# One transfer for the output projection's weights, and one loop of filler matmuls ahead of it, in a decode kernel

## The chip, the cores and the metric

The kernel runs on one core of a Trainium2 chip. The metric is the device time of one execution in microseconds (us), as the median of several runs. A core has five engines, each with its own instruction stream, and they meet only at semaphores: PE (matmuls), DVE and ACT (elementwise work and copies), POOL, and SP, which here issues transfers. Transfers run on 16 DMA rings (one per DMA engine), each of which works off its queue in order.

## The reference, cut to what matters

One token of width 512 goes through a layer norm. Two branches read the result, and everything is added up:

```python
def _A_ref(x, k_cache, v_cache, wq, wo):      # attention, 32 heads on 8 kv heads
    q = (x @ wq).reshape(B, Sq, Hq, Dh)
    k, v = last 4096 positions of the caches, each kv head for 4 heads
    p = softmax(q k * Dh ** -0.5)
    o = p v
    return o.reshape(B, Sq, Hq * Dh) @ wo     # wo: 4096 x 512

def _B_ref(x, w_r, w_gate, w_up, w_down):     # one gated MLP, F = 1792
    r = x @ w_r
    g = silu(x @ w_gate); u = x @ w_up
    y = (g * u) @ w_down                      # w_down: 1792 x 512
    return x + y * sigmoid(r)

xn = layernorm(x)
out = x + _A_ref(xn, ...) + _B_ref(xn, ...)
```

All inputs are bf16. The weights and the two cache windows make 30.67 MB, each byte of which is read once.

## The kernel before

Everything is loaded by transfers that SP issues in this order: wq in two halves, the keys in four pieces of 2 MB, the values in four of 2 MB, w_gate, w_up, then wo in two transfers of 2 MB, and w_down in four pieces of 896, 512, 256 and 128 KB. The place of wo and w_down (`k_sb`) is that of the keys, so SP waits at L407 for DVE to have copied most of them out before it issues these six (L408 to L413, through the helper `dma` at L200, which gives each transfer a semaphore of its own).

In wo, `"(p j) n -> p (j n)"` puts 32 rows of 1 KB, 32 KB in all, on each of 128 partitions. `wo_chunks` cuts these at row 16, so that each transfer has 128 pieces of 16 KB.

PE goes through the stages one after another. The query projection (L300) and the keys' stage (loop at L397, transposes at L380 and scores at L389) come first, then the softmax and the values' stage (loop at L484). Then PE does the gate and up products (L524) and one small matmul, L529, which brings the attention's result into `oT2`. The end of the program is what the change touches:

- `warm(n)` (L189) issues n matmuls of zeros, 128x128 by 128x512, into a PSUM bank that nobody reads; `fill(n)` (L193) is two of them n times. They are called fillers here. They wait for nothing but their turn on PE.
- After L529 come four fillers (`fill(F4)`), and PE waits for `oT2`.
- The loop at L555 goes over the two pieces of wo. For each, PE waits for the piece and issues 16 matmuls (`grouped`, L546). A matmul has one column of `oT2` as its weights and one row of wo, 512 wide, as its moving data; its place `c = j % 4` puts four of them side by side in the array. Between the two pieces a loop of 8 rounds issues 16 fillers.
- When the 32nd matmul is done, DVE adds the four partial sums' bank and the residual (`t_part`, L565). PE issues four more fillers meanwhile.
- The loop at L567 goes over the four pieces of w_down. For each piece PE waits for it and issues two matmuls per row (`by_halves`, L551, 256 wide each). Behind the first piece's 14 it waits for DVE's sum and adds it through the same accumulators with `sel4` as weights.
- DVE and ACT copy the two halves of the result out (L578, L579), and SP writes it.

The order on each engine is the order of the calls in the source.

Of the kernel before, what the change touches and what calls it, by code (L numbers as in the profile page):

```python
# [38 lines left out]
def kernel(  # L39
# [63 lines left out]
    def early(eng, name, out_, in_):  # L103
        s = nc.alloc_semaphore("d_" + name)
        ins = eng.dma_start(out=out_, in_=in_)
        ins.then_inc(s, 16)
        ahead[ins.ins.name] = ins.ins.engine
        return (s, 16)

    t_wq = [early(nc.sync, "wq0", wq_sb[:, 0:KH, :], wq_v[:, 0:KH, :])]  # L110
    t_x = early(nc.scalar, "x", xrow[:], A_x.rearrange("a b d -> (a b) d"))
    W3, F1, F2, F3, F4 = 2, 2, 1, 1, 2

    sb = lambda name, shape, dt: nc.alloc_sbuf_tensor(name, shape, dt)
    HP = HKV // 2
# [71 lines left out]
    te, ac, ve, gp, sy = nc.tensor, nc.scalar, nc.vector, nc.gpsimd, nc.sync  # L187

    def warm(n):  # L189
        for _ in range(n):  # L190
            te.matmul(ps[:, 7, :], lhsT=zst[:], rhs=zmov[:], start=True, stop=True)  # L191

    def fill(n):  # L193
        warm(2 * n)
# [5 lines left out]
    def dma(eng, name, out_, in_):  # L200
        s = S("d_" + name)
        ins = eng.dma_start(out=out_, in_=in_)  # L202
        ins.then_inc(s, 16)
        if name == "v0":
            ends(ins)
        return (s, 16)
# [199 lines left out]

    SP.need((s_c[1], 6))  # L407
    wo_v = A_wo.rearrange("(p j) n -> p (j n)", j=RJ)  # L408
    wo_chunks = [(0, 16), (16, 32)]
    t_wo = [dma(sy, f"wo{k}", wo_sb[:, j0 * D:j1 * D], wo_v[:, j0 * D:j1 * D]) for k, (j0, j1) in enumerate(wo_chunks)]  # L410
    wd_v = B_w_down.rearrange("(p j) n -> p (j n)", j=FB)
    wd_chunks = [(0, 7), (7, 11), (11, 13), (13, 14)]
# [125 lines left out]
                                           in1=ps[:, 3, 0:FC].rearrange("p (i b) -> p b i", b=FB), op0=ALU.mult, op1=ALU.mult))  # L538
    DVE.need(t_h)
    t_hT = DVE.mark(ve.transpose(out=hTr[:].rearrange("p b i -> p (b i)"), in_=h4[:].rearrange("p b i -> p (b i)")))  # L540
    fill(F4)
    PE.need(t_oT2)

    def grouped(j, lhsT, w):
        c = j % 4
        return te.matmul(a_ps[32 * c:32 * c + 1, :], lhsT=lhsT, rhs=w[:, j * D:(j + 1) * D], start=(j < 4), stop=False,  # L546
                         tile_position=(0, 32 * c), skip_group_check=True)
# [7 lines left out]
    for k, (j0, j1) in enumerate(wo_chunks):  # L555
        PE.need(t_wo[k])
        for j in range(j0, j1):
            ins = grouped(j, oT2[:, j:j + 1], wo_sb)
        if k == 0:
            with te.Fori(0, 8):  # L560
                fill(1)
    t_g4 = PE.mark(ins)
    DVE.need(t_g4, t_rf)
    fill(2)
    t_part = DVE.mark(ve.tensor_tensor(out=part, in0=a_ps, in1=rf, op=ALU.add))  # L565
    PE.need(t_hT)
    for k, (j0, j1) in enumerate(wd_chunks):  # L567
# [45 lines left out]
```

## Time and profile before

| what | us |
|---|---|
| median of 8 runs (lowest, highest) | 79.0 (78.72, 79.25) |
| the profiled execution, device time | 78.94 |
| its span, from the first instruction to the last | 77.4 |
| PE busy, of the span | 59.3 |
| DVE busy | 44.0 |
| ACT busy | 30.4 |
| POOL busy | 10.1 |
| data read by DMA | 30.67 MB, 396 GB/s over the span |

The span leaves out some 1.5 us at the two ends of the profiled execution. Busy times are sums over an engine's instructions, without overlap counted twice; matmuls are pipelined, so PE busy does not say how far PE is from its peak. An engine can be busy for much of the span and still set nothing: what counts is what the last instruction waited for. "Issue to landing" of a transfer contains the time it stands in its ring behind others: the four pieces of w_down are issued near 34 us and take some 40 us to land.

### The profile page before, as it was taken

What the parts mean: (1) busy time and instruction counts of PE and PEld (TensorE: products, weight loads), DVE (VectorE), ACT (ScalarE), POOL (GpSimd) and SP (SyncE); (2) the same over time, 40 slices, a digit from 0 to 9 for tenths busy, and PEclk for the clock granted to TensorE, in tenths of its full rate; (3) what the DMA queues carried; (4) which work ended last, traced back from release to release, by engine and by line L of the source; (5) the groups of instructions that cost most, each with busy time, mean ns of one, the idle gap of its engine ahead of it and who ended that gap; (6) DMA issues with size and microseconds to landing.
All of it is one profiled execution on the core that took longest, in us unless ns stands there. A gap on an engine that the chain in (4) does not pass through costs nothing.

```text
span 77.4 us, 1669 instructions
## 1 busy us (share of the span) xinstructions
PE 59.3 (77%) x652; PEld 29.9 (39%) x652; DVE 44.0 (57%) x96; ACT 30.4 (39%) x41; POOL 10.1 (13%) x22
## 2 busy tenths in 40 slices
PE   0015996798898997997995866788887795798891
PEld 0010411336675775685682225222222251343240
DVE  2764900119866957966963762988989248300302
ACT  2771001402895896896775043333343420000001
POOL 3950000000220210220217600000000000000000
PEclk9999999999999999999999999999999999999999
DMA  5999999999999999999999999999989999999910
GB/s 136 389 424 406 406 423 508 423 406 406 415 474 440 415 415 406 432 491 415 410 406 415 432 474 423 415 420 415 459 370 487 422 415 415 423 419 399 379 39 1
DMA packets 2601, 30.72 MB, mean 397 GB/s; under 512 B 291, under 2 KB 422, under 8 KB 806
## 3 DMA queue, kind: packets, MB, share of 16 engines
q1 hardware_dynamic: 2594, 30.67, 94.1%
q8 instruction: 2, 0.03, 0.2%
q14 instruction: 1, 0.01, 0.0%
q10 hardware_dynamic: 4, 0.00, 0.0%
HBM read 30.67 MB, written 0.00 MB: 396 GB/s over the span
## 4 chain that ended last, share of the span: by engine, by line
DMA 70%; PE 14%; ACT 6%; DVE 3%; issue 2%; SPq 1%
DMA k_sb<-in_B_w_down_dram 51%; DMA k_sb<-in_A_k_cache_dram 20%; PE ps L380 8%; ACT kT L352 6%; PE ps L551 3%; PE ps L389 3%; DVE kin L344 2%; SPq L202 1%; DVE kT L349 1%; DVE kT L578 1%; SPq L84 0%; SPq L101 0%
## 5 line engine op out<-in xcount | busy, mean ns | idle before, releaser
L352 ACT COPY kT<-ps 128x1024 bf16<-128x1024 bf16 x19 | 18.6, 1016 | 8.8 <-PE ps L380 8.6
L380 PE MATMUL ps<-perm_bf,kin 128*128 128x128 bf16 x256 | 17.1, 220 | 0.9 <-DVE kin L344 0.4
L380 PEld LDWEIGHTS ps<-perm_bf,kin 128*128 128x128 bf16 x256 | 14.3, 98 | 5.2 <-issue 4.4
L344 DVE COPY kin<-k_sb 128x2048 bf16<-128x2048 bf16 x16 | 11.0, 691 | 4.7 <-DMA k_sb<-in_A_k_cache_dram 4.1
L191 PE MATMUL ps<-zmov,zst 128*128 128x512 bf16 x45 | 11.9, 396 | 1.2 <-PEq L84 1.2
L349 DVE COPY kT<-ps 128x1024 bf16<-128x1024 bf16 x13 | 9.0, 691 | 2.7 <-PE ps L380 2.2
L475 ACT CAST pvS<-ps 128x512 bf16<-128x512 f32 x8 | 4.7, 585 | 10.0 <-PE ps L481 10.0
L389 PE MATMUL ps<-kT,qAB 128*32 128x512 bf16 x68 | 6.8, 389 | 1.9 <-ACT kT L352 1.9
L337 POOL COPY qAB<-qpad 128x64 bf16<-128x64 bf16 x8 | 3.6, 448 | 31.8 <-PE ps L389 31.8
L191 PEld LDWEIGHTS ps<-zmov,zst 128*128 128x128 bf16 x45 | 3.9, 99 | 6.2 <-issue 3.3
L455 DVE COPY vin<-v_sb 128x2048 bf16<-128x2048 bf16 x8 | 5.5, 685 | 1.1 <-PE ps L490 1.0
L461 DVE COPY vin<-v_sb 128x2048 bf16<-128x2048 bf16 x8 | 5.5, 683 | 0.0
L490 PE MATMUL ps<-vin,pTcur 128*32 128x512 bf16 x32 | 3.2, 386 | 2.6 <-ACT pvS L475 2.2
L579 ACT CAST kT<-ps 1x256 bf16<-1x256 f32 x1 | 0.4, 363 | 11.9 <-PE ps L551 11.9
L502 PE MATMUL ps<-zmov,zst 128*128 128x512 bf16 x16 | 4.7, 376 | 0.0
L254 PE MATMUL ps<-ident_bf,xn_row 1*128 1x1 bf16 x4 | 0.3, 165 | 5.2 <-DVE xn_row L249 5.2
L300 PE MATMUL ps<-wq_sb,xnT 128*1 128x512 bf16 x32 | 3.8, 621 | 0.6 <-DMA wq_sb<-in_A_wq_dram 0.6
L565 DVE TENSOR_TENSOR kT<-ps,kT 128x512 f32<-128x512 f32 x1 | 0.7, 692 | 5.6 <-PE ps L546 5.6
L306 ACT CAST q<-ps 128x512 bf16<-128x512 f32 x2 | 1.2, 585 | 5.9 <-PE ps L300 5.9
L496 PE MATMUL ps<-vin,pTcur 128*32 128x512 bf16 x32 | 3.2, 387 | 0.3 <-DVE vin L461 0.2
L490 PEld LDWEIGHTS ps<-vin,pTcur 128*32 128x32 bf16 x32 | 1.1, 92 | 6.0 <-DVE vin L455 5.5
L389 PEld LDWEIGHTS ps<-kT,qAB 128*32 128x32 bf16 x68 | 1.9, 92 | 3.9 <-issue 1.4
(92 smaller groups left out, 52.5 us busy)
## 6 DMA issues: line engine op xcount, KB each, us to landing
k_sb<-in_A_k_cache_dram SPq DMA_DIRECT2D x4, 2048.0 KB, 22.4
v_sb<-in_A_v_cache_dram SPq DMA_DIRECT2D x4, 2048.0 KB, 38.4
wq_sb<-in_A_wq_dram SPq DMA_DIRECT2D x2, 2048.0 KB, 9.1
k_sb<-in_A_wo_dram SPq DMA_DIRECT2D x2, 2048.0 KB, 35.2
wq_sb<-in_B_w_gate_dram SPq DMA_DIRECT2D x1, 1792.0 KB, 42.8
wq_sb<-in_B_w_up_dram SPq DMA_DIRECT2D x1, 1792.0 KB, 46.7
k_sb<-in_B_w_down_dram SPq DMA_DIRECT2D x1, 896.0 KB, 39.1
k_sb<-in_B_w_down_dram SPq DMA_DIRECT2D x1, 512.0 KB, 39.9
```

The costliest lines, as they stand in the source:

```text
L191: te.matmul(ps[:, 7, :], lhsT=zst[:], rhs=zmov[:], start=True, stop=True)
L300: ins = te.matmul(ps[32 * c:32 * c + 1, hf, :], lhsT=xnT[:, kt:kt + 1], rhs=wq_sb[:, kt, (4 * hf + c) * 512:(4 * hf + c + 1) * 512], start ...
L344: ve.tensor_copy(out=kin[:, 2 * h:2 * h + 2, :], in_=k_sb[:, g, 2 * h:2 * h + 2, :]).then_inc(s_c[h], 1)
L349: ve.tensor_copy(out=kT[:, b, :], in_=tp[:, b, :]).then_inc(s_ev[b], 1)
L352: ac.copy(out=kT[:, b, :], in_=tp[:, b, :]).then_inc(s_ev[b], 1)
L380: ins = te.transpose(tp[:, b, k * P:(k + 1) * P], kin[:, b, k * P:(k + 1) * P], perm_bf[:])
L389: ins = te.matmul(sc[32 * cq:32 * cq + 32, e, :], lhsT=qAB[:, e, :], rhs=kT[:, b, :].rearrange("d (k h q) -> d h k q", h=2, q=PH)[:, e], s ...
L455: ve.tensor_copy(out=vin[:, 0].rearrange("p (q k) d -> p q (k d)", q=4), in_=v_in[:, :, 0:4 * DH]).then_inc(s_va, 1)
L461: ve.tensor_copy(out=vin[:, 1].rearrange("p (q k) d -> p q (k d)", q=4), in_=v_in[:, :, 4 * DH:]).then_inc(s_vb, 1)
L475: ac.copy(out=pvS[:].rearrange("p t d -> p (t d)"), in_=pv_ps).then_inc(s_pvs, 1)
L490: ins = te.matmul(pv_ps[32 * tl:32 * tl + 32, :], lhsT=pTcur[:, tl].rearrange("p q e r -> p (q e r)"), rhs=vin[:, 0].rearrange("p (q t) d ...
L502: te.matmul(ps[:, 7, :], lhsT=zst[:], rhs=zmov[:], start=True, stop=True)
```

## The change

`wo_chunks` becomes one piece of 32 rows, so wo is one transfer of 4 MB in 128 pieces of 32 KB, with one semaphore. The loop at L555 then runs once: one wait, and 32 matmuls behind it. The three places with fillers (4, then 16 in a loop between the pieces of wo, then 4) become one loop of twelve rounds of two, 24 again, directly behind L529 and ahead of the wait for `oT2`.

```diff
-    W3, F1, F2, F3, F4 = 2, 2, 1, 1, 2
+    W3, F1, F2, F3 = 2, 2, 1, 1
...
-    wo_chunks = [(0, 16), (16, 32)]
+    wo_chunks = [(0, 32)]
...
-    fill(F4)
+    with te.Fori(0, 12):
+        fill(1)
     PE.need(t_oT2)
...
         PE.need(t_wo[k])
         for j in range(j0, j1):
             ins = grouped(j, oT2[:, j:j + 1], wo_sb)
-        if k == 0:
-            with te.Fori(0, 8):
-                fill(1)
     t_g4 = PE.mark(ins)
     DVE.need(t_g4, t_rf)
-    fill(2)
     t_part = DVE.mark(ve.tensor_tensor(out=part, in0=a_ps, in1=rf, op=ALU.add))
```

## The prediction, made before the changed kernel ran

> **What bounds the kernel now.** I read the page first, for the shares of the engines and of the DMA.
>
> ```profile
> span 77.4 us, 1669 instructions
> DMA  5999999999999999999999999999989999999910
> q1 hardware_dynamic: 2594, 30.67, 94.1%
> DMA 70%; PE 14%; ACT 6%; DVE 3%; issue 2%; SPq 1%
> ```
>
> The DMA row is at nine tenths or more from the second slice to the last but two, and one queue (SP's) carries it all. So the span is the time that 30.67 MB take, plus a short head and tail. The second view is the chain that ended last, in order of time (start, length, what):
>
> ```profile
> 34.09 39.14 DMA k_sb<-in_B_w_down_dram
> 73.23 0.14 issue
> 73.36 1.80 PE ps L551 x26
> 75.16 0.01 issue
> 75.17 0.61 PE ps L551 x6
> 75.78 0.02 issue
> 75.81 0.41 DVE kT L578
> ```
>
> The first piece of w_down, issued at 34.09 and queued behind everything else, lands at 73.23; then PE works the 32 matmuls of L551 off. The third view is the timeline from 64 us on (start, length, engine, line, idle time before it and what ended it):
>
> ```profile
> 64.02 1.02 PE L191 MATMUL ps<-zmov,zst 128*128 128x512 bf16 x4
> 66.28 1.03 PE L546 MATMUL ps<-k_sb,oT 128*1 128x512 bf16 x16 [1.24 <-DMA k_sb<-in_A_wo_dram]
> 67.25 3.63 PE L191 MATMUL ps<-zmov,zst 128*128 128x512 bf16 x16
> 71.08 1.03 PE L546 MATMUL ps<-k_sb,oT 128*1 128x512 bf16 x16 [0.21 <-DMA k_sb<-in_A_wo_dram]
> 72.05 1.04 PE L191 MATMUL ps<-zmov,zst 128*128 128x512 bf16 x4
> 72.17 0.69 DVE L565 TENSOR_TENSOR kT<-ps,kT 128x512 f32<-128x512 f32 x1 [5.56 <-PE ps L546]
> ...
> 74.12 0.60 PE L551 MATMUL ps<-kT,sel 128*1 128x256 f32 x4
> 74.52 0.35 PEld L551 LDWEIGHTS ps<-k_sb,hTr 128*1 128x1 bf16 x8 [0.30 <-DMA k_sb<-in_B_w_down_dram]
> ...
> 75.17 0.09 PEld L551 LDWEIGHTS ps<-k_sb,hTr 128*1 128x1 bf16 x4 [0.31 <-DMA k_sb<-in_B_w_down_dram]
> 75.49 0.08 PEld L551 LDWEIGHTS ps<-k_sb,hTr 128*1 128x1 bf16 x2 [0.23 <-DMA k_sb<-in_B_w_down_dram]
> ```
>
> Inside what the chain calls PE work, PE waits for DMA three more times (0.30, 0.31, 0.23 us): each last piece of w_down is late for it. **The end is set by the last landing**, not by PE. The trace's records of the increments with which the 16 DMA rings report their shares give the landings: gate and up at 56.95 and 61.24, wo at 66.14 and 71.04, w_down at 73.23, 74.47, 75.13 and 75.45. They also show that a landing is that of one late ring: 14 rings end the last piece by 74.15, one at 74.97 and one at 75.45. The latest lost 1.35 us at 23.78, where a 16 KB packet of the instruction queue ran on it (1021 ns, and 1114 ns for the data packet after it); the other 0.86 us after an 8 KB instruction packet at 37.86.
>
> **The change, part by part.** *Transfer.* Two wo transfers of 128 pieces of 16 KB become one of 128 pieces of 32 KB; each ring has 8 packets fewer, and one increment fewer (9 ns). What a packet costs beyond its bytes: packets of 16384, 14336, 7168 and 1024 B took 611, 539, 274 and 46 ns (medians). From 14336 to 7168 B that is 0.0370 ns a byte, which leaves 9 ns a packet; from 16384 to 1024 B 0.0368 and 8 ns; from 16384 to 14336 B alone 0.0352 and 35 ns. So 8 x 8 + 9 = 0.07 us to 8 x 35 + 9 = 0.29 us less on the path. No row has a packet of 32 KB. If the hardware cuts it into two of 16 KB, only the 9 ns go; a loss is bounded by a rate as low as the slowest undisturbed 2 MB step of the queue, 4.91 us against 4.90, two of them 0.02 us. I take 10 ns a packet, **-0.09 us**, because the two wide pairs of sizes agree; ends +0.02 and -0.29.
>
> [...]
>
> *SP's queue.* One issue fewer (0.33 and 0.43 us now) lets the four w_down issues go some 0.4 us earlier, near 33.7. What hides it: the ring is 28 us behind (up lands at 61.24), the last w_down issue stands blocked for 12.85 us, and SP then has nothing until the output at 76.2. Cost 0; if the ring were empty it would be a gain of 0.4.
>
> *The 16 matmuls that ran on the first half.* They now wait for the whole wo, 71.04 - 0.09 = 70.95, and queue behind that wait with the other 16 and all of L551. Four run at a time in the four column groups: 16 take 1.03, a single one 0.378, so a further group of four costs (1.03 - 0.378) / 3 = 0.217, and 32 take 0.378 + 7 x 0.217 = 1.90. They run 71.0 to 72.9. DVE's sum at L565 follows 0.06 later as now, 72.96 to 73.65; it ended at 72.86 before, so it is **0.79 us later**. Who waits for it is the matmul with sel4, fifteenth in PE's order; it began at 74.12, after the 14 of the first w_down piece. That piece lands at 73.14, its 14 matmuls issue until about 73.9, after the sum is ready. So the 0.79 lies in a cover of 74.0 - 72.86 = 1.1 us, and behind it stand the 0.84 us of waits. Cost 0; past the cover each 0.1 us late would first eat those waits.
>
> *The fillers.* 4 + 16 + 4 become 24 in a loop, (16 in 3.63, so 0.217 each) 0.38 + 23 x 0.217 = 5.37 us, 64.02 to 69.4. They end 1.55 us before wo lands; they need not be waited for. The four behind wo, which ran until 73.09, held up nothing (w_down came at 73.23), and gone they give nothing. What they might have protected is the speed of PE. The clock row does not show it: the granted clock is 1.00 throughout, yet the same matmul shape takes 0.63 us early and 0.38 late:
>
> ```profile
> L300 PE MATMUL ps<-wq_sb,xnT x32: 585/631/634, 8.3 to 13.4; 128*1 128x512 bf16 x32
> L546 PE MATMUL ps<-k_sb,oT x32: 377/378/379, 66.3 to 71.7; 128*1 128x512 bf16 x32
> ```
>
> (L300 runs in two groups of 16, 1.88 us each.) After 15 us every matmul is fast, and the emptiest 3.4 us in that part are busy 60% (at 45.5) and 64% (from 63, with the gap of 1.24). After the change the emptiest are 69.4 to 72.8: 1.8 of 3.4 us, 53%. That is only a little outside what was endured; I price it at 0 and keep the slow clock as a rival.
>
> [...]
>
> **Sum.** -0.09 + 0 + 0 + 0. The profiled execution took 78.94 (span 77.4 and 1.5 around it) and would take 78.85; the runs shown have a median of 79.0, 0.06 above it, so **78.9**.
>
> **Rivals.** *First, slower: PE falls to its early speed in the gap before wo.* Place: 69.4 to 71.0. Price: at 1.88 for 16 and 0.63 for one, a group of four costs 0.42, and 32 take 0.63 + 7 x 0.42 = 3.6, so to 74.6; the sum of L565 ends at 75.35 and not 73.65. If PE recovers at once after, L551 has its sel4 (0.4) and 7 more pairs (0.11 each, from 14 in 0.93) left: 76.7 for 75.77, +1.0. If it stays slow, the 14 pairs at 0.21 and sel4 at 0.9 follow from 74.4: 78.3, +2.5. Time 80.0 to 81.5. It decides once L565 ends later than about 74.5 (73.9 plus the waits). For it: the emptiest stretch, and no full-array work after 69.4. Against: 1.24 us of gap and 64% left no mark. Chance 0.11.
>
> *Second, slower: an instruction packet falls on the late ring.* PE's program is 16 instructions shorter and the fetch seen at 74.28 (16 KB, 1264 ns, on a ring that was done) may come at another time. On the latest ring it would cost up to the 1.35 us of the fetch at 23.78, on the next 0.86 - 0.48. Time 79.3 to 80.2. Against: everything up to 64 us is the same code. Chance 0.08.
>
> *Third, faster: the latest ring is not delayed.* The end would be that of the next ring, 0.48 earlier, with the 0.09: 78.4. For it: the fetches hit rings by timing, and one run's trace cannot say how steady that is; against: the one at 23.78 lies long before the change. Chance 0.14.
>
> *Fourth: the change does not do what it says*, the pieces of 32 KB run as two of 16: 79.0. Chance 0.07.
>
> **How the numbers follow.** The forecast keeps 0.60, with its own range of 78.7 to 79.1 (-0.29 and +0.02, and 0.1 for the medians). A measurement of this kernel cannot tell less than about 0.3% (0.24 us) from no change. Of the 0.60, 0.10 lie below 78.76 by the 35 ns, 0.03 above 79.24. Faster: 0.10 + 0.14 = 0.24. Slower: 0.03 + 0.11 + 0.08 = 0.22. Same: 0.47 + 0.07 = 0.54. The range is 78.4 to 79.5: it leaves out the clock rival, half of the second and a little under 78.4, some 0.18.
>
> **What would show it.** Right: the one wo transfer lands near 70.9, 32 matmuls at 0.38 us begin there and end near 72.9, L565 ends near 73.65 and nobody waits for it, the three waits of L551 for w_down are still there, the last w_down piece lands near 75.35. Packets of 32 KB in the records at about 1215 ns confirm the saving; packets of 16 KB the fourth rival. Wrong: matmuls of 0.6 us after 71, a wait of L551 for L565 beyond 74.1, or a last ring that is late by something other than 1.3 us.

## The result, and the profile after

| | before | changed |
|---|---|---|
| median, us (lowest, highest) | 79.02 (78.72, 79.25), 52 runs | 78.78 (78.58, 79.07), 18 runs |
| ratio, 95% interval | | 0.9971 [0.9962, 0.9979] |
| profiled execution, us; its span | 78.94; 77.43 | 78.78; 77.36 |

The changed kernel is 0.24 us faster (0.17 to 0.30). Two more sittings on other occasions gave 0.9989 [0.9978, 1.0000] and 0.9975 [0.9961, 0.9989], so the gain is some 0.1 to 0.3%. The ratios leave out executions over 1.5% above the fastest of their kernel, and those among them in which the granted clock of PE fell (0.978 on average over the span) are counted by themselves below, because they are part of what the change touches.

The page of the changed kernel, the lines that answer to those of before:

```profile
span 77.4 us, 1676 instructions
DMA  5999999999999999999999999999999979799910
...
q1 hardware_dynamic: 2450, 30.67, 94.1%
DMA 71%; PE 14%; ACT 6%; DVE 3%; issue 2%; SPq 1%
```

SP's queue has 144 packets fewer: 128 of data and 16 increments. The DMA row is as full as before but for two sevens between 62 and 68 us, while wo runs, and the shares of the chain are the same to a per cent. The chain's end, in order of time (start, length, what):

```profile
33.66 39.51 DMA k_sb<-in_B_w_down_dram
73.17 0.14 issue
73.30 1.80 PE ps L552 x26
75.10 0.03 issue
75.13 0.59 PE ps L552 x6
75.73 0.02 issue
75.75 0.41 DVE kT L575
```

Each piece lies 0.06 us earlier than before (73.17 for 73.23, 75.75 for 75.81). The w_down issue stands at 33.66 for 34.09, as SP has one issue fewer, and nothing comes of that. The main lines of the changed kernel's timeline from 64 us on:

```profile
64.06 5.34 PE L191 MATMUL ps<-zmov,zst 128*128 128x512 bf16 x24
71.10 1.90 PE L547 MATMUL ps<-k_sb,oT 128*1 128x512 bf16 x32 [1.70 <-DMA k_sb<-in_A_wo_dram]
73.05 0.69 DVE L562 TENSOR_TENSOR kT<-ps,kT 128x512 f32<-128x512 f32 x1 [6.39 <-PE ps L547]
73.30 0.93 PE L552 MATMUL ps<-k_sb,hTr 128*1 128x256 bf16 x14 [0.30 <-DMA k_sb<-in_B_w_down_dram]
74.06 0.60 PE L552 MATMUL ps<-kT,sel 128*1 128x256 f32 x4
74.46 0.35 PEld L552 LDWEIGHTS ps<-k_sb,hTr 128*1 128x1 bf16 x8 [0.30 <-DMA k_sb<-in_B_w_down_dram]
...
75.13 0.09 PEld L552 LDWEIGHTS ps<-k_sb,hTr 128*1 128x1 bf16 x4 [0.33 <-DMA k_sb<-in_B_w_down_dram]
75.43 0.08 PEld L552 LDWEIGHTS ps<-k_sb,hTr 128*1 128x1 bf16 x2 [0.21 <-DMA k_sb<-in_B_w_down_dram]
```

The fillers end at 69.40, PE idles 1.70 us, the 32 matmuls take 1.90 us at full speed, and DVE's sum ends at 73.74, before sel4 wants it at 74.06. The three waits for w_down stand as before (0.30, 0.33, 0.21). So PE still waits for DMA to the end, and the gain in the span is that of the stream.

The stream, that is the work of SP's queue, is best read where only wo differs: from the landing of w_up to the landing of wo, by the increments of the slowest ring (differences taken before rounding). The table has the values of the kernels of the experiments below, too.

| kernel | wo transfers, piece | w_up to wo, us |
|---|---|---|
| before | 2, 16 KB | 61.24 to 71.04: 9.79 |
| e2, e11 (fillers alone) | 2, 16 KB | 9.79, 9.79 |
| e4, e10 | 1, 16 KB | 9.79, 9.79 |
| changed; e5, e9 | 1, 32 KB | 61.25 to 70.97: 9.71; 9.71, 9.72 |
| e1, e3, e8, e12 | 1, 32 KB | 9.71, 9.71, 9.71, 9.72 |
| e7 | 4, 8 KB | 9.93 |

The packets of 32 KB exist and took 1218 ns (median), against 2 x 611. So each of the eight on a ring saves 4 ns by the medians and some 9 ns by the table, and the whole saves 0.07 to 0.08 us. That is about a third of this sitting's gain, and more of the two smaller ones. The rest is what the experiments were for.

### The profile page after: what moved, and what is told of

Its sections match the earlier page's. It is cut to its first block, busy times and chain, and to the rows that moved or that the text cites. A ratio compares the mean times of both kernels' runs of the same rounds, so it can differ in the third digit from the quotient of the medians.

```text
span 77.4 us, 1676 instructions
## 1 busy us (share of the span) xinstructions
PE 58.1 (75%) x652; PEld 30.0 (39%) x652; DVE 43.9 (57%) x96; ACT 30.3 (39%) x41; POOL 10.5 (14%) x22
## 4 chain that ended last, share of the span: by engine, by line
DMA 71%; PE 14%; ACT 6%; DVE 3%; issue 2%; SPq 1%
DMA k_sb<-in_B_w_down_dram 51%; DMA k_sb<-in_A_k_cache_dram 20%; PE ps L380 8%; ACT kT L352 6%; PE ps L552 3%; PE ps L389 3%; DVE kin L344 2%; DVE kT L349 1%; SPq L202 1%; DVE kT L575 1%; SPq L84 0%; SPq L101 0%
## 5 line engine op out<-in xcount | busy, mean ns | idle before, releaser
L300 PE MATMUL ps<-wq_sb,xnT 128*1 128x512 bf16 x32 | 2.9, 500 | 0.7 <-DMA wq_sb<-in_A_wq_dram 0.7
L547 PE MATMUL ps<-k_sb,oT 128*1 128x512 bf16 x32 | 1.9, 378 | 1.7 <-DMA k_sb<-in_A_wo_dram 1.7
```

## Experiments

Unless said otherwise the diffs are against the changed kernel.

**e1: the transfer alone, four fillers left behind wo.**

```diff
-    with te.Fori(0, 12):
+    with te.Fori(0, 10):
         fill(1)
...
     DVE.need(t_g4, t_rf)
+    fill(2)
```

> One transfer of wo as in the changed kernel, but four of the 24 fillers stay behind wo as before, 20 stand ahead. The changed kernel measured -0.24 us (interval -0.17 to -0.30) while the two traces put only -0.07 us on the DMA stream. Packet theory (the gain is the wider pieces alone, and the rest of the -0.24 is how the timing of instruction fetches fell): -0.07 to -0.24, like the changed kernel. Filler theory (the four fillers behind wo cost the missing 0.17): -0.07, so slower than the changed kernel by 0.17. The sum of L565 follows the 32nd matmul by 0.06 either way, and the first w_down matmul starts when its piece lands, near 73.2, or when the four fillers are done, 0.87 after the 32nd matmul, near 73.9, whichever is later: if the second, up to 0.7 of the waits for w_down are eaten, and the end moves little.

Measured: 80.84 us, ratio 1.0234 [1.0212, 1.0256]; neither theory. The row of the granted clock on its page, which is all nines before:

```profile
PEclk9999999999999999999999999999999999995699
```

The stretches of its end (length, then busy time and count on PE, PEld, DVE, ACT, POOL, granted clock, DMA share, GB/s):

```profile
64.40:68.90 4.50, 4.50 (x25) 1.89 (x21) 2.34 (x4) 0.00 (x0) 0.00 (x0) 1.00 0.86 369
68.90:71.20 2.30, 0.03 (x5) 0.05 (x7) 0.00 (x0) 0.00 (x0) 0.00 (x0) 1.00 0.97 400
71.20:74.70 3.50, 3.50 (x33) 1.05 (x34) 0.00 (x0) 0.00 (x0) 0.00 (x0) 0.51 0.70 267
74.70:78.20 3.50, 3.04 (x36) 1.56 (x36) 1.11 (x2) 0.36 (x1) 0.00 (x0) 1.00 0.01 2
```

And of its timeline:

```profile
71.18 3.52 PE L547 MATMUL ps<-k_sb,oT 128*1 128x512 bf16 x32 [2.27 <-DMA k_sb<-in_A_wo_dram]
...
74.74 0.69 DVE L563 TENSOR_TENSOR kT<-ps,kT 128x512 f32<-128x512 f32 x1 [7.70 <-PE ps L547]
75.61 0.63 PEld L552 LDWEIGHTS ps<-k_sb,hTr 128*1 128x1 bf16 x14 [0.42 <-DVE kT L563]
```

This is the prediction's first rival, met by accident: with 20 fillers ahead the gap before wo is 2.26 us and not 1.70. The clock records of this trace put half clock from 71.30 to 74.71, exactly 3413 ns. In the 3413 ns before that PE was busy from 67.88 to 68.92 and from 71.18, 34% of the time. The 32 matmuls took 3.52 us (the rival's sum: 3.6), DVE's sum ended at 75.43 (the rival: 75.35), DMA waits vanish from L552, and the end lies at 78.2 for 76.2. All four executions have a granted clock of 0.978 or 0.979 on average, which is what one such stretch makes (half of 3.413 us is 0.0215 of the span of 79.4 us). The full clock came back after it, and the price was +1.9 us against before, four fillers behind wo included, between the rival's +1.0 and +2.5. As a test of the transfer by itself the run is lost.

**e2 and e11: the fillers alone.** Two transfers, all 24 fillers ahead.

```diff
-    wo_chunks = [(0, 32)]
+    wo_chunks = [(0, 16), (16, 32)]
```

> Two transfers of 16 KB pieces as before, all 24 fillers ahead of wo as in the changed kernel. Packet theory: 0.0 against before (78.97 to 79.07), as the stream is the same and PE waits for it. Filler theory: -0.17, most of the change's gain. Program-length theory (a PE program 15 instructions shorter moves instruction fetches): -0.17 too, to be told apart by the padded kernel.

> Two transfers of 16 KB pieces, all fillers ahead, none behind. Stream theory: as before, +0.0 (in the first six it was +0.1). Clock theory: in the first six, one execution ran with the granted clock at 0.978 on average and took 80.33, because between the 16th matmul and w_down PE is busy 45% of the emptiest 3.4 us; so one or two in twelve again at 80.2 to 80.6, none in the changed kernel (emptiest 50%), and none in before but at the very end. If the clock theory is wrong, no execution here falls.

Measured: 1.0014 [0.9997, 1.0030] and 0.9999 [0.9980, 1.0018], so the place of the fillers is no gain. But of the 18 executions two took 80.33 and 80.14, both with the granted clock at 0.978. (A third fell at 14.6 us, and one of 73 of before at some time, 79.00 and 78.76 us, without cost.) In e2's trace, without fillers behind the first half of wo and behind the second, PE has 2 x 1.03 us of work between 69.5 and 73.4 and is busy 45% of the emptiest 3.4 us there (the length of e1's half clock); in e11's trace PE comes 0.5 us later, and the emptiest there is 57%. In before the 16 fillers between the halves and the four behind wo fill these gaps. The clock theory expected one or two in twelve at 80.2 to 80.6 and got one at 80.14. For the two slow executions the place of the fall isn't on record; that it lies here, and not early like the costless one, is inferred from what they lost.

**e3: the program as long as before.** Eight fillers written out instead of four rounds.

```diff
-    with te.Fori(0, 12):
+    with te.Fori(0, 8):
         fill(1)
+    fill(4)
```

> The changed kernel with the 24 fillers as eight rounds of two and eight written out, so that PE's program is as long as before (16 instructions more than in the changed kernel), and the same work runs in the same order. Packet theory and filler theory: as the changed kernel, -0.24. Program-length theory: back to -0.07.

Measured: 0.9988 [0.9973, 1.0003], -0.09 us (-0.21 to +0.02). Taken alone this is near the program-length theory's -0.07, and -0.24 lies just outside. But the changed kernel itself came to -0.09 and -0.20 us by the ratios of its later sittings (e5, e9), so the run doesn't separate the theories. Its stream step is that of the changed kernel, 9.71.

**e4 and e10: one transfer, pieces of 16 KB.** Each partition's 32 rows land as two blocks with a gap of a row.

```diff
-    wo_sb = k_flat[:, FB * D:(FB + RJ) * D]
+    wo_sb = k_flat[:, FB * D:(FB + RJ + 2) * D]
...
+    HB = RJ // 2 * D
+    t_wo.append(dma(sy, "wo0", wo_sb.rearrange("p (h n) -> p h n", h=2)[:, :, 0:HB], wo_v.rearrange("p (h n) -> p h n", h=2)))
...
-rhs=w[:, j * D:(j + 1) * D]
+rhs=w[:, (j + j // 16) * D:(j + j // 16 + 1) * D]
```

> The changed kernel with one transfer of wo whose pieces are 16 KB: each partition's 32 rows land as two blocks of 16 with a gap of one row between. Packet theory: 16 packets of 611 ns a ring again, one increment of 9 ns fewer: within 0.02 of before in the stream, so -0.01, or -0.17 if the part that the stream does not explain comes from the fillers' place or the program. If the whole -0.24 is from one transfer less (a cost for each transfer that the packet records do not show), this one has it all: -0.24.

> One transfer of wo in pieces of 16 KB, all fillers ahead: the changed kernel but for the width of the pieces. In the first trace wo took 9.78 us from the landing of w_up here, 9.80 before and 9.72 changed. Width theory: +0.07 us in the span against the changed kernel. Outside the span: with one transfer 1.40, as in the changed kernel, if the second part of the gain comes from the number of transfers; 1.49 if it comes from the width of the pieces.

Measured: 0.9997 [0.9981, 1.0012] and 0.9997 [0.9974, 1.0021]. The second holds one execution of 79.91 with the clock at 0.978; the other eleven average 78.92, beside 78.86 for the changed kernel (e9) and 79.05 for before in the same sitting. The stream step is that of 16 KB pieces (9.79, 9.79) and not the changed kernel's 9.71: it is the width of the pieces that saves in the stream, not the number of transfers.

**e5 and e9: the changed kernel again.**

> The changed kernel as it is, beside before on the same chip, to tell its -0.24 us (52 runs against 18) from the scatter between sittings. Stream theory: wo takes 9.72 us from the landing of w_up instead of 9.80 (8 packets of 32 KB at 1217 ns against 16 of 16 KB at 611), so -0.08 in the span. Outside theory: the time outside the span was 1.48 on average for before (two wo transfers; 1.52 in the kernel with the fillers alone) and 1.40 for the changed kernel (1.39 and 1.44 in the other two with one transfer), so another -0.08, -0.16 in all. If neither is all, -0.24 again.

> The changed kernel a third time, the measure for the three runs beside it. So far -0.29% (interval -0.38 to -0.21) and -0.11% (-0.22 to 0.00) against before. Stream theory: -0.08 us in the span, -0.1%. With the part outside the span (1.41 on average with one wo transfer, 1.49 with two, so -0.08): -0.2%, 78.85 where before has 79.0.

Measured: 0.9989 [0.9978, 1.0000] and 0.9975 [0.9961, 0.9989]. The difference of times splits into span and rest. Over the executions at full clock, with their spans to a tenth of a us:

| kernel (executions) | mean span | mean time outside it |
|---|---|---|
| before, beside e1 to e4 (10), e5 to e8 (27), e9 to e12 (35) | 77.49, 77.53, 77.56 | 1.48, 1.49, 1.49 |
| e2 (5), e11 (10): two transfers, fillers ahead | 77.52, 77.52 | 1.54, 1.48 |
| changed (20), e5 (12), e9 (12) | 77.41, 77.47, 77.45 | 1.40, 1.42, 1.41 |
| e3 (6): changed, longer program | 77.42 | 1.44 |
| e4 (6), e10 (11): one transfer, 16 KB | 77.53, 77.51 | 1.39, 1.41 |
| e8 (11): four fillers behind | 77.79 | 1.41 |
| e7 (9): four transfers, 8 KB | 77.64 | 1.46 |
| e12 (12): wq in one transfer too | 77.64 | 1.41 |

Beside before in the same sitting, the changed kernel (e5, e9) has 0.06 and 0.11 us less in the span, and 0.07 and 0.08 less outside it. Single spans scatter by 0.10 to 0.14 us, so each of the two span differences is uncertain by some 0.04, and the stream's 0.07 to 0.08 fits both.

The time outside is no smooth shift but a step. In the profiled executions, whose spans are known to a ns, it is 1.51 us in before, e2 and e7, and 1.41 to 1.42 in the other eleven (e11, with two transfers, among them). Over all executions on record with their spans, it is above 1.465 in 57 of 91 with two wo transfers (before, e2, e11), and in 4 of 95 with one (3 of these in e3 and e5); in e7 with four it is 4 of 12, in e6 with eight 3 of 6. So with two transfers some six of ten executions end about 0.1 us later, and with one hardly any.

**e7: four transfers, pieces of 8 KB.**

```diff
-    wo_chunks = [(0, 32)]
+    wo_chunks = [(0, 8), (8, 16), (16, 24), (24, 32)]
```

> Fillers as in the changed kernel, wo in four transfers of 8 rows, pieces of 8 KB: 32 packets of 8 KB a ring. From the medians of 7168 B (274 ns) and 16384 B (611) one of 8 KB takes some 311, so wo takes 32 x 311 + 4 x 9 = 9.99 us from the landing of w_up. Stream theory: +0.27 in the span against the changed kernel, +0.19 against before. Outside theory: +0.24 more against the changed kernel outside the span. The sum of L565 follows the last eight matmuls and is no later than now.

Measured: 79.15 us, 1.0013 [0.9994, 1.0033]; nine executions at full clock average 79.11, and three of twelve had it at 0.978 and took 80.18 to 80.59. PE is busy 43% of its emptiest 3.4 us, as the matmuls are spread further (24 by 71.0, eight from 71.2, and then nothing until 73.5). The packets took 313 ns, and wo 9.93 us against 9.99 expected: +0.22 in the stream against the changed kernel, +0.18 in the mean span. Outside the span stand 1.46, not 1.64: a price for each transfer is refuted.

**e6: eight transfers of 16 partitions.**

```diff
+    t_wo8 = [dma(sy, f"wo{k}", wo_sb[16 * k:16 * k + 16, :], wo_v[16 * k:16 * k + 16, :]) for k in range(8)]
...
-        PE.need(t_wo[k])
+        PE.need(*t_wo8)
```

> The changed kernel with wo in eight transfers of 16 partitions each, pieces of 32 KB: the same 128 packets of 32 KB, seven increments a ring and seven issues more. Stream theory: 7 x 9 ns = +0.06 in the span against the changed kernel, nothing outside it. Outside theory (0.08 us outside the span for each transfer): +0.56 outside the span, total 79.3 to 79.5. [...]

Measured: 108.35 us, 1.3679 [1.3622, 1.3737]; no theory had it. The page of this kernel, the DMA rows and the group that waited for wo (busy, mean ns, idle time before it and its releaser behind the last two bars):

```profile
DMA  6999999999999999999999992995959929289500
GB/s 190 397 453 422 422 459 404 446 428 422 452 397 452 416 413 452 397 452 412 430 428 428 198 177 24 196 135 61 171 61 159 171 24 183 32 154 309 219 13 0
...
L549 PE MATMUL ps<-k_sb,oT 128*1 128x512 bf16 x32 | 3.6, 627 | 24.6 <-DMA k_sb<-in_A_wo_dram 24.6
```

The packets of 32 KB took 4402 ns (median) and not 1218, 112 of the 128 between 4.1 and 4.7 us: 7.4 bytes a ns on a ring, 119 GB/s on 16. From the start of wo's first packet to the end of its last, 59.1 to 97.9 us, it is 108 GB/s. What made them slow no run here shows. For the question it was meant for, the run says nothing.

**e8: four fillers behind wo again, 24 ahead kept.**

```diff
     DVE.need(t_g4, t_rf)
+    fill(2)
```

> The changed kernel with 28 fillers: its 24 ahead of wo and the four behind it as before. In the run with 20 ahead the clock fell to half in the gap of 2.26 us before wo and hid what the four cost; here the gap is 1.70 as in the changed kernel and the clock should stay. The sum of L565 ends at 73.75 as in the changed kernel. The four end 0.87 us after the 32nd matmul, near 73.9 instead of 73.0, so the 14 matmuls of the first w_down piece start 0.6 late and sel4 at 74.7 instead of 74.06; the waits for w_down (0.30, 0.33, 0.21) are eaten but for about 0.2. Waits theory: 0 to +0.1 us against the changed kernel. If the four are what the change's gain came from: +0.15 to +0.25.

Measured: 79.23 us, 1.0028 [1.0015, 1.0042], on average +0.31 against the changed kernel beside it (79.20 and 78.89), more than the waits theory's 0 to +0.1. The clock stayed in all eleven. Its timeline:

```profile
72.85 1.04 PE L191 MATMUL ps<-zmov,zst 128*128 128x512 bf16 x4
...
73.81 0.93 PE L552 MATMUL ps<-k_sb,hTr 128*1 128x256 bf16 x14
...
74.58 0.60 PE L552 MATMUL ps<-kT,sel 128*1 128x256 f32 x4
...
75.01 0.93 PE L552 MATMUL ps<-k_sb,hTr 128*1 128x256 bf16 x14
75.98 0.36 ACT L577 CAST kT<-ps 1x256 bf16<-1x256 f32 x1 [12.02 <-PE ps L552]
```

No bracket with a DMA wait stands at L552 any more: sel4 is 0.52 late, all 0.84 us of waits are eaten, and PE ends at 75.94, 0.6 after the last landing at 75.31 and not 0.3. PE has become the bound. So the four fillers cost nothing in before and 0.3 us behind a single transfer.

**e12: wq in one transfer of 32 KB pieces, too.**

```diff
-    t_wq = [early(nc.sync, "wq0", wq_sb[:, 0:KH, :], wq_v[:, 0:KH, :])]
+    t_wq = [early(nc.sync, "wq0", wq_sb[:], wq_v)] * 2
...
-    t_wq.append(dma(sy, "wq1", wq_sb[:, KH:, :], wq_v[:, KH:, :]))
```

> The changed kernel with wq too in one transfer of 32 KB pieces (two of 16 KB before): the same saving at the head of the queue. Stream theory: another 8 x 5 + 9 = 0.05 to 0.08 us, every later landing earlier by that, 78.75 to 78.8 where the changed kernel has 78.85. The 16 query matmuls that ran on wq's first half at 8.3 wait for the whole, near 12.2, and the 32 end near 14.2 to 15.8 (at the clock of 0.38 or 0.63 us each) instead of 13.3 to 14.1; what hides it is the first keys, which land at 17.1. Rival: PE is then idle from 8.3 to 12.2 and warms up later, the keys' stage starts slow, but keys and values end long before their weights land, so the end does not move: 0.

Measured: 79.02 us, 1.0001 [0.9981, 1.0020], 0.19 slower on average than the changed kernel beside it. Its timeline:

```profile
66.67 5.34 PE L191 MATMUL ps<-zmov,zst 128*128 128x512 bf16 x24
71.94 1.90 PE L546 MATMUL ps<-k_sb,oT 128*1 128x512 bf16 x32
73.66 0.93 PE L551 MATMUL ps<-k_sb,hTr 128*1 128x256 bf16 x14
```

The query stage runs 12.3 to 17.0, the keys' stage starts at 20.5 for 17.9, and that delay is carried through every stage of PE: L528 is at 66.63 for 64.03. The keys and values do not wait for their data that long, so nothing hides it. The 24 fillers then end after wo has landed (71.1), and as in e8 PE is the bound. What the stream may have saved at its head can't be seen.

## Why the prediction was right, and where it was off

- **What bounds the kernel**: right. The three waits for w_down stand in the profile after, and the two kernels that eat them (e8, e12) are the two that lose to the changed kernel by PE's work.
- **The transfer, -0.09 us on the path**: right in kind and near in size. The stream shows -0.07 to -0.08, and by width alone -0.07 (changed, e5 and e9 against e4 and e10). The low fixed part of a packet (8 to 9 ns, for 4 to 9 measured) was the right one of the two; the 35 ns of the one odd pair of sizes was not. A fixed time for each queued transfer isn't seen: the two wo landings of before stand 4.90 us apart, and 8 packets of 611 ns make 4.89.
- **The sum, 78.85 for the profiled execution and 78.9 for the median**: measured 78.78 and 78.78. The moved median is -0.24, over two and a half times the term. That it lies inside the forecast's own range (78.7 to 79.1) is owed to that range's width, which stood for 35 ns a packet and the scatter of medians, and to that extent it is luck. The step that was mis-sized is the sum itself: it held the 1.5 us around the span constant, and these measured 0.07 to 0.08 less on average with one wo transfer. The spans carry another 0.06 to 0.11. That leaves 0.05 to 0.11 of the first sitting's 0.24, which is about what the sittings differ among each other.
- **What shortens the time outside the span stays open.** It goes with one wo transfer, wide pieces or not (e4, e10), fillers behind or not (e8), and with two it is long in 10 of 18 executions with all fillers ahead, too (e2, e11). It doesn't grow with the number of transfers (1.46 with four, 1.41 with wq merged too), e3 is an unclear case (1.44, long in 2 of 6), and no trace covers it.
- **The 16 matmuls that have to wait**: right. 1.90 us at full clock, DVE's sum at 73.74 for a predicted 73.65, sel4 without a wait.
- **The four fillers behind wo, "gone they give nothing"**: right against before (e2, e11), but it hid two couplings. With one transfer they must go, or they cost 0.31 us (e8). With two transfers and with these four and the 16 between the halves all ahead, 2 of 18 executions lost time at the lower clock (80.33 and 80.14 us, e2 and e11); which of the two groups matters was not tested. The prediction priced each part beside before alone.
- **The clock rival**: didn't happen in any of the 44 executions of the changed kernel; e1 showed it to be real, at the place and nearly the price given (3.52 us for 3.6). That PE's share is to be read over 3.4 us was not shown when the prediction was made; half clock in e1 lasted 3413 ns. The margin is small: 24 fillers leave a gap of 1.52 to 1.70 us in the three traces of the changed kernel (1.55 was predicted) and it did not fall, 20 leave 2.26 and all four executions fell. Of 18 executions with the same PE work behind 16 KB pieces (e4, e10), one did.
- **Instruction packets**: in the changed kernel's trace the packet that makes the last ring late ran at 30.45 us and not at 23.78, and the ring is late by 1.2 us at the end, before by 1.3. The third and the second rival found nothing to act on.

## What to carry to other kernels

Where a queue of transfers sets the end, wide pieces are worth their fixed part, here some 9 ns for each packet saved on a ring (0.07 to 0.08 us for eight), and splitting one transfer into narrower ones over all 128 partitions cost just that (e7; a split by partitions cost 29 us, e6); the price of either is read from the packets' durations by size. Fillers are to be placed anew whenever a wait moves: the same four behind wo were free with two transfers and cost 0.3 us with one, where the work behind them no longer waited for data (e8), and the clock fell with a gap of 2.26 us ahead of wo (e1) and not with 1.70 (changed). Test the neighbours of a filler count before trusting it: four moved from ahead of wo to behind it cost 1.9 us here.

## What the hardware showed that was not expected

- Half clock came for exactly 3413 ns and followed a stretch of that length in which PE was busy 34% (e1's trace). With 43 to 45% in the emptiest such stretch of the trace (e2, e7) executions at the lower clock that also lost time came in 2 of 18 (e2 and e11) and 3 of 12; in the kernels whose traces show 48% and more in 1 of 79 (changed, e3, e4, e8, e10), and that one was of e10, which has the 48%.
- The lengths of full clock in these traces are 16, 18 and 19 times 3413 ns (54.61 us in e1, 61.44 in e2, 64.85 in before), and they begin at 16.68, 16.31 and 14.24 us. e7 kept full clock after a stretch of 3413 ns that was busy 46% (71.05 to 74.46) and e2 lost it after one of 44% (74.33 to 77.75). But e11 lost it after one of 52% (11.18 to 14.59), so the busy share of such a stretch alone doesn't tell in these runs, and no limit follows from them. The gap before wo also differs: 1.03 to 1.77 us in the seven traces with these 24 fillers ahead of one transfer.
- One instruction packet of 16 KB, at 22.7 to 35.5 us, makes its ring 1.1 to 1.5 us late in all 14 traces: the transfer in work is the first whose last increment comes by that much after the bulk. The ring didn't catch up: in every trace but e6's each later transfer's last increment is late by 1.1 to 1.5 us, to the end.
- By their packets of 32 KB, the 16 rings moved 119 GB/s together when each transfer covered 16 neighbouring partitions (e6, 4402 ns a packet), and 430 when it covered 128 (changed, 1218 ns).
